# Moving the loads of pairs seven and eight behind the fourth pair's bit rows in a fused hash attention and gated MLP kernel

## The chip, the cores and the metric

The kernel runs on one core of a Trainium2 chip. The metric is the device time of one execution in microseconds, as the median of several runs. A core has a matrix engine (PE, with its weight loads shown as PEld), a vector engine (DVE), a scalar engine for activations (ACT), a general engine (POOL) and a sync engine (SP) that here issues nearly all DMA transfers. The engines run side by side, each works through its own instructions in program order, and semaphores order them against each other. The transfers themselves run on 16 DMA engines.

## The reference

There are 4 batches of 8 heads, 768 positions and 64 features. Every query and key is hashed into a bucket of six bits by the signs of six projections. A query attends only to keys in its own bucket. The result goes through a gated MLP with 512 inputs and 1536 hidden units.

```python
q_bits = (np.einsum('bhsd,dk->bhsk', q, proj) > 0).astype(np.int64)
k_bits = (np.einsum('bhsd,dk->bhsk', k, proj) > 0).astype(np.int64)
q_bucket = np.sum(q_bits * powers, axis=-1)
k_bucket = np.sum(k_bits * powers, axis=-1)
mask = q_bucket[:, :, :, None] == k_bucket[:, :, None, :]
scores = np.where(mask, scale * np.matmul(q, k.transpose(0, 1, 3, 2)), -1e9)
attn = softmax(scores)              # over the keys
attn_out = np.matmul(attn, v)
...
x = attn_out.transpose(0, 2, 1, 3).reshape(B * S, H * D)
g = x @ w_gate
gelu = 0.5 * g * (1.0 + erf(g / sqrt(2)))
ffn_out = gelu * (x @ w_val) @ w_out
out = x + sigmoid(x @ w_res) * ffn_out
```

## The kernel before, in words

**Pairs.** The 32 heads are worked on as 16 pairs, four pairs to a batch, numbered 0 to 15 in the code (so "pair seven" of the title is index 6, and "the fourth pair" is index 3). For each pair, `load` (L87) issues one transfer for the queries (side 0), one for the keys (side 1) and one for the values (side 2) from SP. Queries and keys are held in three buffers per side, so that pair 6 takes the buffer of pair 3 and pair 7 that of pair 4.

**From load to scores.** Queries and keys go two ways. On the first, `cast` (L191, POOL) makes them bf16, `transpose_dma` (L208, issued from SP) turns them so that the features lie on partitions (tile `aug`), and `move_second` (L212, POOL) copies the second head's half into the tile `second`. On the other way, `blocks` (L242, DVE) transposes the float32 data in blocks of 32 into `t32` (five buffers), and `hash_half` (L274, PE) multiplies them with the projections, in two halves of the feature dimension, into one PSUM tile. After the second half a DVE instruction (L287) turns the sums into signs. From index 4 on, two pairs are hashed together: `hash_half` of 4 covers pairs 4 and 5, that of 6 covers 6 and 7. `spread` (L293) is four DVE shuffles that bring the signs into rows, and `mask_rows` (L322) is four transfers of 10.5 KB each that lay these seven rows (the "bit rows") beside the transposed features: two into `second` and two into `aug`, in this order. The scores are then one matmul over features and bit rows together, and a bucket that differs costs so much that the exponential is nought.

**The order.** The program is written out by hand as 147 chunks ("slots"). In each, `scores` (L436) issues the score matmuls of one chunk and its exponential on ACT; then come the tasks that `at(slot, function, ...)` (L529) has put down for this slot, in the order in which they were put down; and then, by `flush`, the products with the values of the chunk two places earlier. The first pair has 12 chunks, the others have 9 each. `base(p)` is the first slot of pair p: `b1`, `b2` and `b3` in the code are the slots 12, 21 and 30, and `base(4)` is slot 39. A task's slot fixes only its place in its engine's order, and for transfers the place in SP's order; when it runs is set by semaphores.

**What follows.** Three chunks into a batch, `gate_val` (L450) does the first half of the MLP for the batch before it, in 12 steps, as one block of PE work; the second half (`project`, L475) is cut into single matmuls that fill the PE between the chunks of the next batch. The MLP weights come in by `load_w` (L175, 512 KB each, four staging buffers, issued on SP) and are cast to bf16 by `cast_w` on POOL. The first four are issued at slot b2 + 1, the next four at b3 + 1.

The tasks that the change moves are put down in the lines L636 to L674. Around them stand, in SP's order: the bit rows of pair 2, the transposes of pair 3 and the values of pair 3 (L635 to L638); the loads of pairs 6 and 7 (L639, L653); the bit rows of pair 3 (L654); the values and transposes of pair 4 (L657, L659); four weight loads (L662); the values of pair 5 (L664); the bit rows of pair 4 (L672).

Of the kernel before, what the change touches and what calls it, by code (L numbers as in the profile page):

```python
# [17 lines left out]
def kernel(  # L18
# [498 lines left out]
    def base(p):  # L517
        return order.index((p, 0))
# [10 lines left out]
    def at(slot, f, *args):  # L529
        if f in (hash_half, transpose_pe):  # L530
            uses_tp.add(slot)
        tasks[slot].append(lambda: f(*args))
        busy[slot] += cost.get(f, 0.0)
# [88 lines left out]
    b1, b2, b3 = (base(i) for i in (1, 2, 3))  # L622
# [13 lines left out]
    for side in range(2):  # L636
        at(b1 + 3, transpose_dma, (3, side))
    at(b1 + 3, load, 3, (2,))  # L638
    at(b1 + 3, load, 6, (0, 1))  # L639
    at(b1 + 2, blocks, (3, 1))  # L640
    at(b1 + 2, blocks, (4, 0))
    at(b1 + 4, blocks, (4, 1))
# [6 lines left out]
    for side in range(2):  # L649
        at(b1 + 6, move_second, (3, side))  # L650
        at(b1 + 7, cast, (5, side))
        at(b1 + 7 + side, blocks, (5, side))
    at(b1 + 7, load, 7, (0, 1))  # L653
    at(b1 + 8, mask_rows, 3)  # L654
    at(b1 + 8, values_prep, 3)

    at(b2, load, 4, (2,))  # L657
# [9 lines left out]
    for a in range(4):  # L667
        at(b2 + 6 + a // 2, spread, 4, a)

    for i, s in enumerate((b2 + 2, b2 + 7, b2 + 8, b3 + 2)):  # L670
        at(s, blocks, (6 + i // 2, i % 2))
    at(b3, mask_rows, 4)  # L672
    for dh, s in enumerate((b3 + 4, b3 + 6)):
        at(s, hash_half, 6, dh, ROW)  # L674
    for i in range(NWS):
        at(b2 + 5 + i, cast_w)
# [120 lines left out]
```

## Time and profile before

| | |
|---|---|
| median of 5 runs | 348.92 us (348.65 to 351.32) |
| time of the profiled execution | 348.92 us |
| its span, first to last instruction | 347.1 us |
| PE busy, share of the span | 335.7 us, 97% |
| ACT busy | 210.3 us, 61% |
| DVE busy | 153.2 us, 44% |
| POOL busy | 153.1 us, 44% |
| transfers issued through SP's queue | 43.56 MB, 45.3% of the 16 DMA engines |
| first scores of pairs 1, 2, 3 and 4 | about 20, 30, 40 and 50 us |

An engine that is busy in the profile is not always at its peak: the ends of the matmuls are modelled. The shares are means over stages that differ. In the first 50 us the program works on batch 0 alone and has no MLP matmuls to fill the PE with; afterwards blocks of `gate_val` (about 54 to 86 us for the first one) alternate with attention of the next batch, filled with MLP matmuls. In lines of a timeline the first number is the start in us, the second the time from the first start to the last end, and what stands in brackets is how long the engine was idle before it and what ended that. "SPq" rows are the issuing instructions on SP, not the transfers.

### The profile page before, as it was taken

To read this page: it belongs to the slowest core of one execution; us is meant where nothing else is said; L and a number is where in the kernel's file an instruction comes from. 1 tells how busy PE (TensorE), PEld (TensorE's weight loads), DVE (VectorE), ACT (ScalarE), POOL (GpSimd) and SP (SyncE) were. 2 spreads that over 40 slices of the span, in tenths; PEclk is the share of its full clock that TensorE was granted. 3 is DMA by queue.
4 is the path that set the end of the run, shared out by engine and by line. 5 is a ranking of instruction groups with operands and counts; after the bars stand their busy time and mean duration, and the time that the engine had idled before them with its cause. 6 is when DMAs were issued, how large, how long until landed. Compare 5 with 4: busy or idle time off the path is not lost.

```text
span 347.1 us, 7432 instructions
## 1 busy us (share of the span) xinstructions
PE 335.7 (97%) x2961; PEld 197.1 (57%) x3010; DVE 153.2 (44%) x280; ACT 210.3 (61%) x238; POOL 153.1 (44%) x198
## 2 busy tenths in 40 slices
PE   8999989999999999999999999999999999999995
PEld 4545656655565566566456556566556565656443
DVE  5997823334136526343444446343452025334243
ACT  5888986334898886223888788323788884332220
POOL 6898575865479496200068579300038222000000
PEclk9999999999999999999999999999999999999999
DMA  7966999896806973730014783600003321000012
GB/s 227 275 229 190 284 340 199 290 343 175 261 17 161 207 215 79 190 115 2 0 37 126 185 204 105 145 23 1 2 3 89 59 55 60 2 0 2 30 60 91
DMA packets 52718, 44.04 MB, mean 127 GB/s; under 512 B 31657, under 2 KB 44621, under 8 KB 52685
## 3 DMA queue, kind: packets, MB, share of 16 engines
q1 hardware_dynamic: 52540, 43.56, 45.3%
q8 instruction: 23, 0.38, 0.5%
q14 instruction: 11, 0.08, 0.1%
q0 software_dynamic: 64, 0.02, 0.0%
q10 hardware_dynamic: 80, 0.00, 0.0%
HBM read 29.36 MB, written 6.29 MB: 103 GB/s over the span
## 4 chain that ended last, share of the span: by engine, by line
PE 84%; ACT 4%; DVE 4%; POOL 4%; issue 2%; DMA 2%; DVEq 0%; ACTq 0%; POOLq 0%
PE sp L463 35%; PE fps L498 16%; PE sp L441 13%; PE av L412 8%; PE rps L483 5%; PE hs L282 4%; ACT e L445 4%; DMA aug<-bits 2%; PE wps L188 1%; POOL ldv L338 1%; POOL va L332 1%; DVE x_tok L389 1%; POOL o L507 1%; DVE o L504 1%; PE tp L398 1%
## 5 line engine op out<-in xcount | busy, mean ns | idle before, releaser
L445 ACT ACTIVATE e<-sp 128x1024 bf16<-128x1024 f32 (+1 forms) x147 | 143.5, 1008 | 25.5 <-PE sp L441 22.3
L469 ACT ACTIVATE gt<-sp 128x768 bf16<-128x768 f32 x48 | 38.9, 810 | 83.0 <-PE sp L463 83.0
L470 DVE SCALAR_TENSOR_TENSOR hh<-gt,sp 128x768 bf16<-128x768 bf16 x48 | 45.8, 954 | 81.4 <-PE sp L463 81.4
L498 PE MATMUL fps<-wo,hh 128*128 128x512 bf16 (+2 forms) x285 | 74.3, 369 | 1.3
L463 PE MATMUL sp<-x_sb,wg 128*128 128x256 bf16 (+1 forms) x376 | 70.3, 325 | 0.4
L463 PE MATMUL sp<-x_sb,wv 128*128 128x256 bf16 (+1 forms) x376 | 69.8, 325 | 0.6 <-DVE hh L470 0.2
L412 PEld LDWEIGHTS <-e 128*128 128x128 bf16 x1152 | 50.1, 97 | 33.2 <-issue 9.3
L441 PE MATMUL sp<-aug,aug 71*128 71x512 bf16 x192 | 54.3, 326 | 2.9 <-ACT e L445 1.7
L412 PE MATMUL av<-va,e 128*128 128x65 bf16 x1152 | 56.0, 193 | 0.6
L463 PEld LDWEIGHTS <-wv 128*128 128x128 bf16 x384 | 37.5, 98 | 25.2 <-issue 0.4
L463 PEld LDWEIGHTS <-wg 128*128 128x128 bf16 x384 | 37.2, 98 | 24.4
L441 PE MATMUL sp<-second,second 128*128 128x256 bf16 (+1 forms) x174 | 47.4, 320 | 0.2
L507 POOL TENSOR_TENSOR o<-o,x_tok 128x512 f32<-128x512 f32 x18 | 20.8, 1155 | 56.2 <-DVE o L504 49.3
L498 PEld LDWEIGHTS <-hh 128*128 128x128 bf16 x300 | 28.6, 97 | 27.0
L504 DVE SCALAR_TENSOR_TENSOR o<-th,fps 128x512 f32<-128x512 f32 (+2 forms) x25 | 16.5, 662 | 52.9 <-PE fps L498 34.7
L389 POOL TENSOR_TENSOR x_tok<-total,rec 128x768 bf16<-128x768 f32 x9 | 13.2, 1472 | 45.0 <-DVE rec L388 45.0
L214 POOL COPY second<-aug 64x768 bf16<-64x768 bf16 x29 | 23.6, 825 | 19.5 <-DMA aug<-nat 17.8
L245 DVE STREAM_TRANSPOSE t<-ld 128x768 f32<-128x768 f32 (+1 forms) x34 | 29.5, 904 | 3.7 <-DMA ld<-in_q_dram 2.2
L486 ACT ACTIVATE th<-rps 128x512 f32<-128x512 f32 x24 | 14.3, 596 | 18.7 <-PE rps L483 14.3
L483 PE MATMUL rps<-wr,x_sb 128*128 128x512 bf16 x96 | 24.6, 379 | 0.0
L441 PEld LDWEIGHTS <-second 128*128 128x128 bf16 x192 | 18.6, 98 | 5.3 <-issue 2.3
L441 PEld LDWEIGHTS <-aug 71*128 71x128 bf16 x192 | 16.2, 97 | 6.6 <-issue 1.8
(71 smaller groups left out, 233.8 us busy)
## 6 DMA issues: line engine op xcount, KB each, us to landing
ldv<-in_v_dram SPq DMA_DIRECT2D x16, 384.0 KB
out_dram<-o SPq DMA_DIRECT2D x23, 256.0 KB
ld<-in_q_dram SPq DMA_DIRECT2D x15, 384.0 KB
ld<-in_k_dram SPq DMA_DIRECT2D x15, 384.0 KB
ws<-in_moe_w_gate_dram SPq DMA_DIRECT2D x6, 512.0 KB
ws<-in_moe_w_val_dram SPq DMA_DIRECT2D x6, 512.0 KB
ws<-in_moe_w_out_dram SPq DMA_DIRECT2D x6, 512.0 KB
ws<-in_moe_w_res_dram SPq DMA_DIRECT2D x2, 512.0 KB
```

What stands on the lines that cost most here:

```text
L214: eng.tensor_copy(second[x[0] % NM][x[1]][D:P], aug[x][D:P])
L245: nc.vector.transpose(t32[x][:, c0:c1].rearrange("p c h n -> p (c h n)"), raw[x][:, c0:c1].rearrange("p c d -> p (c d)"))
L412: nc.tensor.matmul(o[:, qt0 + i, :], e[:, off + i * P:off + (i + 1) * P], va[:, hi, jt, 0:D + 1], start=(hi not in begun), stop=(jt == T - ...
L441: nc.tensor.matmul(sp[:, off:off + nq * P], ks[0:n, jt, :], qs[0:n, qt0:qt0 + nq, :], start=True, stop=True)
L445: nc.scalar.activation(e[:, 0:n], sp[:, 0:n], AF.Exp, scale=float(ALPHA))
L463: nc.tensor.matmul(sp[:, c0:c1], w[:, kk, bass.ts(m, P)], xs[:, kk, c0:c1], start=(kk == 0), stop=(kk == KM - 1))
L469: nc.scalar.activation(gt, sp[:, 0:S], AF.Gelu)
L470: nc.vector.scalar_tensor_tensor(hh[:, m, :], gt, 0.5, ps[1][:, 0:S], op0=ALU.mult, op1=ALU.mult)
L483: nc.tensor.matmul(rps, x_sb[b][:, kk, t, :], wr[:, kk, :], start=(kk == 0), stop=(kk == KM - 1))
L498: nc.tensor.matmul(fps, hh[:, m, bass.ts(t, P)], wo[:, m, cs], start=(m == 0), stop=(m == KF - 1))
L504: nc.vector.scalar_tensor_tensor(o[:, cs], th[:, cs], 1.0, fps, op0=ALU.add, op1=ALU.mult)
L507: last.tensor_add(o3, o3, x_tok[b][:, k0:k1, t, :])
```

## The change

Three things are put in other places; no instruction is added or taken away. (1) The loads of queries and keys of pair 6 (they stood at slot b1 + 3) and of pair 7 (at b1 + 7) are both put at b1 + 8, and the bit rows of pair 3 move from b1 + 8 to b1 + 7, so that on SP they are issued ahead of these four loads. (2) The four `blocks` of pairs 6 and 7 move from the slots b2 + 2, b2 + 7, b2 + 8 and b3 + 2 to b2 + 6, b2 + 8, b3 + 2 and b3 + 3. (3) The two hash halves of pairs 6 and 7 move from b3 + 4 and b3 + 6 to b3 + 5 and b3 + 7.

```diff
@@ -636,7 +636,6 @@
     for side in range(2):
         at(b1 + 3, transpose_dma, (3, side))
     at(b1 + 3, load, 3, (2,))
-    at(b1 + 3, load, 6, (0, 1))
     at(b1 + 2, blocks, (3, 1))
     at(b1 + 2, blocks, (4, 0))
     at(b1 + 4, blocks, (4, 1))
@@ -650,8 +649,9 @@
         at(b1 + 6, move_second, (3, side))
         at(b1 + 7, cast, (5, side))
         at(b1 + 7 + side, blocks, (5, side))
-    at(b1 + 7, load, 7, (0, 1))
-    at(b1 + 8, mask_rows, 3)
+    at(b1 + 7, mask_rows, 3)
+    for i in (6, 7):
+        at(b1 + 8, load, i, (0, 1))
     at(b1 + 8, values_prep, 3)
 
     at(b2, load, 4, (2,))
@@ -667,10 +667,10 @@
     for a in range(4):
         at(b2 + 6 + a // 2, spread, 4, a)
 
-    for i, s in enumerate((b2 + 2, b2 + 7, b2 + 8, b3 + 2)):
+    for i, s in enumerate((b2 + 6, b2 + 8, b3 + 2, b3 + 3)):
         at(s, blocks, (6 + i // 2, i % 2))
     at(b3, mask_rows, 4)
-    for dh, s in enumerate((b3 + 4, b3 + 6)):
+    for dh, s in enumerate((b3 + 5, b3 + 7)):
         at(s, hash_half, 6, dh, ROW)
     for i in range(NWS):
         at(b2 + 5 + i, cast_w)
```

## The prediction, before the change was run

> **What bounds the kernel now.** I read the page first, then the chain of waits, then the queue and engine timelines around 20 to 60 us, where every edit lies. The profiled execution took 348.92 us, the same as the median of the five runs shown; 347.1 us of it is the span. The sum below is made against 348.92.
>
> The page, with its 40 slices of 8.68 us:
>
> ```profile
> span 347.1 us, 7432 instructions
> ...
> DMA  7966999896806973730014783600003321000012
> ```
>
> The DMA engines are 90% busy in the slices from 34.7 to 60.7 us and little used after 60. PE has only 6.8 us of gaps in the whole span (gaps between its rows added up), so from the first MLP stage (about 54 us) on it is full: a stall of PE before that is not won back later, it moves the end one to one. The question is therefore what decides when batch 0 is over. The chain of waits between 9 and 60 us (start, us, what):
>
> ```profile
> 40.53 0.59 PE sp L441 x2
> 41.13 0.26 PE av L412 x8
> 41.39 0.84 POOL second L214
> ...
> 44.64 5.34 DMA aug<-bits
> 49.98 0.05 issue
> 50.03 0.62 PE sp L441 x2
> ```
>
> Until 40 us the chain runs through the exponentials on ACT. Then it leaves the engines: the fifth pair (index 4) cannot begin its scores before its bit rows have landed, and this small transfer, issued at 44.64, lands at 49.98. The engines around it:
>
> ```profile
> 50.03 0.39 PE L441 MATMUL sp<-aug,aug 71*128 71x512 bf16 x1 [0.73 <-DMA aug<-bits]
> ```
> ```profile
> 50.73 2.86 ACT L445 ACTIVATE e<-sp 128x1024 bf16<-128x1024 f32 x3 [0.56 <-PE sp L441]
> ```
> ```profile
> 40.62 1.59 POOL L214 COPY second<-aug 64x768 bf16<-64x768 bf16 x2 [3.82 <-DMA aug<-nat]
> ```
>
> PE stands 0.73 us, ACT 0.56 us. So at this one place the DMA queue is already the bound, by 0.56 us. Why does a 10.5 KB transfer take 5.34 us? By SP's timeline four weight loads of 512 KB (issued 39.32 to 41.4) and a value load lie ahead of it, and these lie behind the two transposes, and these behind the loads that the change moves:
>
> ```profile
> 29.82 0.59 SPq L95 DMA_DIRECT2D ldv<-in_v_dram  x1
> 30.46 0.46 SPq L95 DMA_DIRECT2D ld<-in_q_dram  x1
> 31.02 0.41 SPq L95 DMA_DIRECT2D ld<-in_k_dram  x1
> 31.54 0.40 SPq L95 DMA_DIRECT2D ld<-in_q_dram  x1
> 32.04 0.41 SPq L95 DMA_DIRECT2D ld<-in_k_dram  x1
> 32.54 1.51 SPq L329 DMA_DIRECT2D second<-bits  x2
> 34.16 1.48 SPq L329 DMA_DIRECT2D aug<-bits  x2
> 35.69 0.44 SPq L95 DMA_DIRECT2D ldv<-in_v_dram  x1
> 36.69 2.58 SPq L209 DMA_TRANSPOSE aug<-nat  x2
> ```
>
> The stretches (last columns: DMA share, GB/s) show that from 32 us on the engines never run dry:
>
> ```profile
> 31.00:32.00 1.00, 0.87 (x13) 0.60 (x11) 1.00 (x2) 1.00 (x2) 0.64 (x1) 1.00 0.74 152
> 32.00:33.00 1.00, 1.00 (x10) 0.29 (x8) 0.97 (x3) 1.00 (x2) 0.91 (x2) 1.00 1.09 394
> 33.00:34.00 1.00, 1.00 (x9) 0.29 (x8) 0.70 (x1) 0.36 (x1) 1.00 (x3) 1.00 1.00 369
> ```
>
> The trace's semaphore increments tell when each transfer landed (median of its engines): value load 33.0, loads of pair 6 at 34.0 and 35.0, of pair 7 at 36.3 and 37.4, pair 3's bit rows by 38.3, value load of pair 4 39.56, transposes 40.4 and 41.2, weights 43.0 to 47.1, value load 48.2, bit rows of pair 4 49.0 (their last engine 49.98). It is one line of work from 32 to 50.
>
> **The change, part by part.**
>
> Loads behind the bit rows of pair 3. SP issues the same four loads and four bit-row transfers, in the other order; SP's own time is unchanged. The bit rows need the last of four shuffles, which ends at 30.85 (DVE, 30.50 + 0.35), and the copies of the second head, which end at 30.95 and 32.18 (POOL); the second kind gates only the two aug transfers. Four took 32.54 to 35.64, 3.10 us, so now 30.95 to 34.05. The first load is issued at 34.1 instead of 30.46, the value load at 36.1 and the transposes at 36.6, as before. But the DMA engines have nothing large between 33.3 and the first bytes of that load. The nearest row is the value load issued at 18.21 on an empty queue: it landed at 21.3, 3.07 later. So pair 6's first load lands at 37.2; the next loads follow at 1.02 each (22.32, 23.34, 24.36, 25.36 in the same burst): 38.2, 39.2, 40.2, the value load of pair 4 at 41.25 instead of 39.56. **Late by 1.7 us**; at the 1.12 us that the four loads took here (34.04 to 37.40) by 2.0. Part may come back: between the transposes (41.2) and the first weight load (43.0) lie 1.9 us where the later weight loads are 1.34 apart, so 0.4 to 0.5 us are dry there now, and with a queue that is behind they would be filled. That gives 1.3 at least, 2.0 at most; I take **1.6 us**, near the middle, as nothing speaks for either end.
>
> What is late next: the transposes land at 42.1 instead of 40.4, POOL's copies (40.62) follow, behind them on POOL pair 4's values (42.28 to 45.25) and the weight casts, each 1.6 later. First use of these values is after the scores of pair 4, which are late too. The second group of weights is cast by 57.4; its first use is the fifth of twelve MLP steps, about 53.8 + 4 x 2.6 = 64.2: 7 us of cover. Without it 1.6 us would be paid again. Bit rows of pair 4 land at about 51.6, and PE starts that pair at 51.65 instead of 50.03.
>
> Bit rows of pair 3 1.6 us earlier: worth nothing. They landed by 38.4, and pair 3 starts at 40.53 in a row of nine exponentials without a pause (36.62 to 45.07).
>
> Blocks later. Four DVE transposes of 0.92, same number. One wait goes:
>
> ```profile
> 35.60 0.98 DVE L245 STREAM_TRANSPOSE t<-ld 128x768 f32<-128x768 f32 x1 [1.90 <-DMA ld<-in_q_dram]
> ```
>
> Behind it stood the sign step of pairs 4 and 5 (36.50), whose matmuls had ended at 35.72, so up to 0.8 us is gained there; now a block stands between two pairs of shuffles, 0.92 lost. The shuffles still end near 39.6, and SP reaches pair 4's bit rows at 42.21. I take 0; the cover is 2.6 us, and without it -0.8 to +0.9.
>
> Hash halves one chunk later: eight matmuls each, 0.78. The first half now falls into the chunk that also holds six PE transposes (0.5). ACT stands 0.49 and 0.54 us at 45.55 and 48.13 after the halves now. This could save both or double both: -1.0 to +1.0, all before the bit rows land, with the last exponential of pair 3 ending at 50.17 against bit rows at 51.6. I take 0, covered by 1.4. The hash itself is used by shuffles a whole pair later.
>
> Sum: 348.92 + 1.6 = **350.5 us**, PE's gap at that pair 0.73 + 1.6 = 2.3 us.
>
> The granted clock is 1.00 in every one of these stretches, beside a gap of 0.73 us. The Trainium skill's TensorE page (TensorE: Matmul & The Clock Gate, section Why this matters for your kernels) warns against PE gaps over about 3 us, after which the clock is halved. The gap worked out here stays under that, so by the rule the sum is the same; only the deep case below would cross it, and by the rule another 1.7 us (an estimate: half of a 3.4 us window) would come on top there. No gap here is that long, so the trace can't confirm it.
>
> **Rivals.**
>
> 1. *The delay is taken up.* All of the dry time before the weights is refilled (the 1.3 above), and the one DMA engine that makes the bit rows land 1.0 us after the other six (49.98 against 49.05) falls elsewhere: 1.3 - 1.0 = +0.3: 349.2. For it: such late engines come and go (loads at 34.04 had one engine at 35.58). Against: the weight stream is full, and nothing says where the late one falls.
>
> 2. *Deeper.* A late engine adds to the hole. After an instruction fetch of 16 KB that took 1.04 us on one engine, that engine's share of the next five loads was 1.0 to 1.5 late. If the bit rows sit on one that is late by this more than now, 1.6 + 1.0 to 1.5 = 2.6 to 3.1: **351.8 us**. It decides if the last of the bit rows lands after 52.5.
>
> 3. *Faster.* The load's delay is hidden and the shorter waits on DVE and ACT count: bit rows land before 50.0, ACT goes straight on at 50.17, saving its 0.56, and the two pauses of 0.49 and 0.54 go with the moved hash: 348.92 - 1.6 = 347.3 at best, 348.4 with the first alone. It decides only if the queue is not behind at all at 41 us, and the landings above say that it is.
>
> That the order on SP doesn't change is excluded: one queue, in program order.
>
> **How the numbers follow.** Forecast 0.52, its own range 349.9 to 351.2; taken up 0.17; deeper 0.23; faster 0.08. What a measurement of this kernel can tell is about 0.5%, 1.74 us: 347.2 and 350.66. Slower than that: four tenths of the forecast's case and the deep one, 0.22 + 0.23 = 0.45. Faster: half of the last, 0.05 with rounding. The rest, 0.50, is the same. Range 348.9 to 351.9: it leaves out the faster case and the upper half of the deep one.
>
> **What would show it.** Right: on SP the four bit-row transfers start near 31 and the first of the four loads near 34; DMA share well under 0.5 from 34 to 36; POOL's copies of pair 4 near 42.3; PE's wait for aug<-bits at pair 4 near 2.3 us at 51.6; the gate and value matmuls start 1.6 later and everything behind them by the same. Wrong in size: a wait of another length there. Wrong in kind: no wait for bit rows at pair 4, or a difference that arises after 60 us; also DVE waiting for a load again, which would make the hash late.

## The result, and the profile after

The changed kernel is slower: a median of 352.59 us over 23 runs, against 348.82 us over 44 runs of the kernel before. The ratio of the two kernels on record is 1.0081, with a 95% interval of 1.0061 to 1.0102, that is 2.8 us (2.1 to 3.6). The medians lie further apart, 3.8 us: the changed kernel's executions took longer where their granted clock was lower (348.6 to 349.9 us at 0.998 or more, 352.7 and more at 0.990), and the two slowest, 355.21 and 355.73 us, are not in the ratio. Its profiled execution took 351.38 us with a span of 349.6.

First the head of the page of the changed kernel and the rows of its 40 slices (8.74 us each) for the granted clock and the DMA engines:

```profile
span 349.6 us, 7430 instructions
...
PEclk9999998999999999999999999999999999999999
DMA  7965999798724972850003793510002311000012
```

The fourth DMA slice (26 to 35 us) has 5 where the kernel before had 6, and the seventh slice of the clock, 52 to 61 us, shows 8 instead of 9. The kernel before shows 9 in every slice of the clock. Next the chain of waits between 30 and 60 us (start, us, what):

```profile
35.20 8.39 DMA aug<-nat
...
43.74 0.61 POOL second L214
...
44.51 0.84 POOL second L214
...
47.68 4.00 DMA aug<-bits
...
51.73 0.93 PE sp L441 x2
```

In the kernel before the chain ran through ACT until 40 us. Now it leaves ACT at 35.2 and goes through the transposes of pair 4, the copies, and the bit rows of pair 4. The engines at the same place, PE first, then ACT, then POOL:

```profile
51.73 0.50 PE L441 MATMUL sp<-aug,aug 71*128 71x512 bf16 x1 [3.67 <-DMA aug<-bits]
```
```profile
52.76 1.02 ACT L445 ACTIVATE e<-sp 128x1024 bf16<-128x1024 f32 x1 [3.82 <-PE sp L441]
```
```profile
43.74 1.59 POOL L214 COPY second<-aug 64x768 bf16<-64x768 bf16 x2 [8.01 <-DMA aug<-nat]
```

PE's wait for the bit rows of pair 4 has grown from 0.73 to 3.67 us, and POOL's for the transposes from 3.82 to 8.01. SP's queue shows the new order:

```profile
29.45 1.49 SPq L329 DMA_DIRECT2D second<-bits  x2
31.05 1.50 SPq L329 DMA_DIRECT2D aug<-bits  x2
32.60 0.44 SPq L95 DMA_DIRECT2D ld<-in_q_dram  x1
33.10 0.45 SPq L95 DMA_DIRECT2D ld<-in_k_dram  x1
33.59 0.47 SPq L95 DMA_DIRECT2D ld<-in_q_dram  x1
34.11 0.47 SPq L95 DMA_DIRECT2D ld<-in_k_dram  x1
34.62 0.47 SPq L95 DMA_DIRECT2D ldv<-in_v_dram  x1
35.20 6.22 SPq L209 DMA_TRANSPOSE aug<-nat  x2
```

And the stretches of 1 us (last three columns: granted clock, DMA share, GB/s):

```profile
32.00:33.00 1.00, 1.00 (x21) 0.73 (x20) 0.00 (x0) 0.76 (x2) 1.00 (x3) 1.00 0.04 11
33.00:34.00 1.00, 1.00 (x12) 0.16 (x8) 0.00 (x0) 0.80 (x2) 0.91 (x2) 1.00 0.38 58
...
37.00:38.00 1.00, 1.00 (x16) 0.79 (x13) 1.00 (x4) 1.00 (x3) 0.00 (x0) 1.00 0.86 192
38.00:39.00 1.00, 0.91 (x13) 0.50 (x10) 1.00 (x5) 1.00 (x3) 0.00 (x0) 1.00 0.79 221
...
41.00:42.00 1.00, 0.94 (x18) 0.63 (x18) 1.00 (x3) 1.00 (x2) 0.00 (x0) 1.00 0.58 39
42.00:43.00 1.00, 0.92 (x13) 0.65 (x12) 0.91 (x2) 1.00 (x2) 0.00 (x0) 1.00 0.53 112
...
52.00:53.00 1.00, 1.00 (x12) 0.70 (x11) 0.00 (x0) 0.24 (x1) 0.30 (x1) 0.50 1.07 414
```

There are two holes in the DMA stream where the kernel before had one line of work: the expected one at 32 to 34 us, where the loads have not been issued yet, and a second at 41 to 43; at 37 to 39 the stream is slower too. The half clock begins as PE's gap ends and lasts from 51.9 to 55.3.

**Where the time went.** The two profiles start differently (pair 1's first exponential is at 20.71 before and at 19.76 after, which no part of the change touches), so I count from that exponential. The first Gelu comes 35.43 us after it before and 39.01 us after it now: +3.58. From the first Gelu to the end it is 291.00 and 290.83 us. Thus 3.58 - 0.95 - 0.17 = 2.46 us, which is the difference of the spans, and all of the loss lies ahead of the first Gelu.

### The profile page after: what moved, and what is told of

It reads as the page before. It is cut to its first block, busy times and chain, and to the rows that moved or that the text cites. A ratio compares the mean times of both kernels' runs of the same rounds, so it can differ in the third digit from the quotient of the medians.

```text
span 349.6 us, 7430 instructions
## 1 busy us (share of the span) xinstructions
PE 334.8 (96%) x2961; PEld 197.2 (56%) x3010; DVE 153.3 (44%) x280; ACT 210.1 (60%) x238; POOL 153.0 (44%) x198
## 4 chain that ended last, share of the span: by engine, by line
PE 81%; DMA 5%; POOL 4%; ACT 3%; DVE 3%; issue 2%; SPq 0%; POOLq 0%; DVEq 0%; ACTq 0%
PE sp L463 35%; PE fps L498 15%; PE sp L441 13%; PE av L412 8%; PE rps L483 5%; PE hs L282 4%; ACT e L445 3%; DMA aug<-nat 2%; DMA aug<-bits 1%; DMA ld<-in_q_dram 1%; POOL ldv L338 1%; POOL va L332 1%; DVE x_tok L389 1%; POOL o L507 1%; POOL second L214 1%
## 5 line engine op out<-in xcount | busy, mean ns | idle before, releaser
L445 ACT ACTIVATE e<-sp 128x1024 bf16<-128x1024 f32 (+1 forms) x147 | 143.3, 1008 | 29.3 <-PE sp L441 24.7
L412 PEld LDWEIGHTS <-e 128*128 128x128 bf16 x1152 | 50.8, 98 | 33.3 <-issue 9.4
L463 PEld LDWEIGHTS <-wv 128*128 128x128 bf16 x384 | 37.6, 98 | 25.2 <-issue 0.3
```

Source lines behind the costliest of these rows:

```text
L412: nc.tensor.matmul(o[:, qt0 + i, :], e[:, off + i * P:off + (i + 1) * P], va[:, hi, jt, 0:D + 1], start=(hi not in begun), stop=(jt == T - ...
L445: nc.scalar.activation(e[:, 0:n], sp[:, 0:n], AF.Exp, scale=float(ALPHA))
L463: nc.tensor.matmul(sp[:, c0:c1], w[:, kk, bass.ts(m, P)], xs[:, kk, c0:c1], start=(kk == 0), stop=(kk == KM - 1))
```

## The experiments

HOLE is the theory that the late loads leave the DMA engines empty, so that the transposes and bit rows of pair 4 come late and PE's clock drops after the wait. TASKS is the rival that the moved blocks and hash halves do it. "Gelu" is the time in us from pair 1's first exponential to the first Gelu in the profile, "gap" the longest idle time of PE, in us, between 30 and 55 us of the profile and what ended it.

| run | ratio to before, 95% | Gelu | gap |
|---|---|---|---|
| before | 1 | 35.43 | 0.73, bit rows of pair 4 |
| changed | 1.0081 (1.0061 to 1.0102) | 39.01 | 3.67, bit rows of pair 4 |
| e1 loads only | 1.0074 (1.0046 to 1.0102) | 39.06 | 2.08, division of pair 2 |
| e2 blocks and hash only | 0.9991 (0.9965 to 1.0017) | 35.30 | 0.90, exponential on ACT (bit rows of pair 4 landed just then, too) |
| e3 only pair 7's loads late | 0.9990 (0.9965 to 1.0015) | 35.21 | 0.81, bit rows of pair 4 |
| e4 filler | 1.0064 (1.0040 to 1.0089) | 37.71 | 0.47, exponential on ACT |
| e5 changed, bits first | 0.9997 (0.9974 to 1.0020) | 35.09 | 0.32 |
| e6 changed, transposes first | 1.0076 (1.0041 to 1.0110) | 37.71 | 1.57, division of pair 2 |
| e7 before, bits first | 0.9993 (0.9968 to 1.0017) | 35.18 | 0.89, bit rows of pair 3 |
| e8 changed, both first | 1.0021 (0.9997 to 1.0045) | 37.53 | 1.52, division of pair 2 |
| e9 e8 with later blocks | 0.9952 (0.9928 to 0.9976) | 34.37 | 0.32 |
| e10 e6 with later blocks | 1.0068 (1.0036 to 1.0100) | 38.54 | 2.95, bit rows of pair 4 |
| e11 e7 with the change's blocks | 0.9984 (0.9961 to 1.0007) | 35.38 | 0.85, bit rows of pair 3 |
| e12 changed, bits from POOL | 1.0084 (1.0056 to 1.0113) | 40.45 | 3.65, bit rows of pair 3 |

### e1 and e2: the change in its two halves

e1 is the changed kernel with

```diff
-    for i, s in enumerate((b2 + 6, b2 + 8, b3 + 2, b3 + 3)):
+    for i, s in enumerate((b2 + 2, b2 + 7, b2 + 8, b3 + 2)):
...
-    for dh, s in enumerate((b3 + 5, b3 + 7)):
+    for dh, s in enumerate((b3 + 4, b3 + 6)):
```

and e2 is the kernel before with this edit turned round.

> Only the loads are moved behind the bit rows of pair 3; blocks and hash halves stand where they stood before. Theory HOLE (the DMA engines run empty ahead of the late loads, so the transposes, weight loads and bit rows of pair 4 land late, and PE then stands so long that its clock falls): as slow as the whole change, +2.8 to +3.8 us on the kernel before, with a wait of PE for aug<-bits at pair 4 of 3 to 4 us. Rival TASKS (the later blocks and hash halves push the chunks of pair 3 back): at most +0.5 us. One thing could add to it: the block of pair 6 again waits on DVE for its load, about 4 us, with pair 4's sign step behind it; the bit rows of pair 4 are issued later than that, so HOLE expects no cost from it.

> Only the blocks and the hash halves of pairs 6 and 7 are moved; the loads stay in front. HOLE: the same time as before within 0.5 us, PE's wait at pair 4 again 0.5 to 1.0 us. TASKS: slower by 2 us or more.

The loads alone lose as much as the whole change, the blocks and hash halves alone lose nothing that can be told: TASKS falls. But in e1 the loss sits in another place than HOLE said. DVE waits for pair 6's load, and behind it stands the division of pair 2, which frees the accumulator that pair 3's products need. DVE's rows of e1, then PE's:

```profile
36.05 0.98 DVE L245 STREAM_TRANSPOSE t<-ld 128x768 f32<-128x768 f32 x1 [4.07 <-DMA ld<-in_q_dram]
...
42.41 0.96 DVE L389 TENSOR_TENSOR x_tok<-av,rec 128x768 bf16<-128x768 f32 x1
```
```profile
43.51 1.04 PE L412 MATMUL av<-va,e 128*128 128x65 bf16 x16 [2.08 <-DVE x_tok L389]
```

This gap of 2.08 us costs more than itself, for the clock is at 0.50 from 42.4 to 49.3 us. The bit rows of pair 4 landed at 52.31 in e1 and PE came to them at 52.5, so there was no wait left. One lateness on two paths: with the blocks in their old place the late load holds PE by way of DVE, with the blocks later it holds it by way of the bit rows. The two do not add up, for the second hides behind the first.

### e3: half of the loads

The changed kernel with the loads of pair 6 in front again:

```diff
     at(b1 + 3, load, 3, (2,))
+    at(b1 + 3, load, 6, (0, 1))
...
-    for i in (6, 7):
-        at(b1 + 8, load, i, (0, 1))
+    at(b1 + 8, load, 7, (0, 1))
```

> The whole change, but the loads of pair 6 go back in front of pair 3's bit rows (slot b1 + 3); only those of pair 7 stay behind them. HOLE: the loads of pair 6 keep the DMA engines busy until about 35, those of pair 7 are issued at 34.6 and would land at 37.7 on an empty queue against 36.3 before, so the hole is 1.0 to 1.5 us instead of 2 to 3.4: +0.2 to +1.5 us on the kernel before, PE's wait at pair 4 between 0.7 and 2.2 us, clock whole. If the order against the bit rows as such counted, and not the empty stretch, it would be half of the change's loss or more: +1.4 us up.

The loss is gone, not halved. The transposes of pair 4 still landed 1.1 us later than before (20.84 against 19.73 us after the first exponential), but the bit rows 0.2 us earlier. The first 1.1 us of lateness are taken up on the way (dry time ahead of the weights, one late DMA engine), as the prediction's first rival had it; only what is over that arrives.

### e4: the clock

```diff
+        if (p, c) == (HP, 0):
+            warm_up(14, 4)
         new = scores(p, c)
```

> The whole change, with 14 matmuls of 512 columns on constants (3.0 us at full clock, results not used) put in front of the first scores of pair 4, where PE stands for 3.67 us. If the halved clock after that gap costs what the rows of the changed kernel say (52 to 56 us at 0.50, first Gelu 7.0 us after the pair's first score against 6.1 before), this is 0.9 us faster than the changed kernel, its granted clock is 1.00 throughout, and the wait for aug<-bits shrinks by the 3 us while the pair starts at the same time. If the clock costs nothing (ACT being the bound there), it is the same as the changed kernel within 0.3 us.

PE's rows of e4 show the filler, and the wait behind it:

```profile
47.93 3.19 PE L188 MATMUL wps<-eps_sb 128*128 128x512 bf16 x14
51.40 0.39 PE L441 MATMUL sp<-aug,aug 71*128 71x512 bf16 x1 [0.28 <-DMA aug<-bits]
```

The clock is 1.00 throughout. From PE's first score of pair 4 to the first Gelu it is 6.11 us, as in the kernel before, against 7.04 in the changed one: the half clock costs **0.93 us** there, in this pair of profiles. The rest of the 1.3 us that e4's Gelu is earlier is a bit row that landed earlier in this execution. The medians (351.15 against 352.59) point the same way; the intervals of the two ratios overlap.

### e5 and e7: the bit rows of pair 4 ahead of 1.4 MB

In the changed kernel (e5) and in the one before (e7):

```diff
-    for i in range(NWS):
+    for i in range(2):
         at(b2 + 1, load_w)
...
-    at(b2 + 6, load, 5, (2,))
...
     at(b3, mask_rows, 4)
+    for i in range(2):
+        at(b3, load_w)
+    at(b3, load, 5, (2,))
...
-        at(b2 + 5 + i, cast_w)
-        at(b3 + 1, load_w)
+        at((b2 + 5, b2 + 6, b3 + 2, b3 + 3)[i], cast_w)
+        at(b3 + 1 + i // 2 * 3, load_w)
```

> The whole change, and the bit rows of pair 4 are issued ahead of two of the four weight loads (the value side's) and of the values of pair 5, so that 1.4 MB less lies in front of them; these loads and their casts come behind, and the second group's value side behind pair 5's transposes. Theory HOLE says that the loads of pairs 6 and 7 cost only by way of these bit rows: they land about 3.3 us earlier (48.4 against 51.7 in the changed kernel's profile), PE's wait at pair 4 falls from 3.7 to under 0.6 us, the clock stays whole, and the time is 3.5 to 4.2 us below the changed kernel, -0.5 to +0.3 us on the kernel before. If the late loads cost by another way too (pair 6's data, POOL, the weights), 1 us or more of the loss stays.

> The kernel before, with the same reordering of pair 4's bit rows ahead of two weight loads and pair 5's values. If the bit rows hold PE in the kernel before as well (0.73 us, ACT 0.56), they now land near 46, the wait is gone and the time is 0.3 to 0.8 us lower; if the later weight loads come too late for the first gate matmuls, it is higher by what PE waits there, up to 2 us.

e5 is HOLE's plainest test: the loads are as late as in the change, and the loss is gone. In the changed kernel, with its blocks later, they cost by way of pair 4's bit rows; beside e7, which has the same edit with the loads early (0.9997 and 0.9993), a cost by another way can't be told. The profile alone is less clear, for behind the first Gelu it is 0.7 us longer than before (291.69 against 291.00), and no run here tells why. ACT's rows of e5 go through pair 4's start (49.36, four exponentials in a row) after 0.65 us of idle time where the changed kernel has 3.82:

```profile
46.77 1.94 ACT L445 ACTIVATE e<-sp 128x1024 bf16<-128x1024 f32 x2 [0.67 <-PE sp L441]
49.36 3.97 ACT L445 ACTIVATE e<-sp 128x1024 bf16<-128x1024 f32 x4 [0.65 <-PE sp L441]
```

e7 took the wait at pair 4 away too, but the gain can't be told from nothing. In its profile PE waits one pair earlier, for the bit rows of pair 3, which lie behind the early loads:

```profile
39.06 0.38 PE L441 MATMUL sp<-aug,aug 71*128 71x512 bf16 x1 [0.89 <-DMA aug<-bits]
```

So the old order can have a cost of its own. In the profile shown of before it was not there.

### e6, e8, e9 and e10: the transposes of pair 4 ahead of the late loads

e6 is the changed kernel with

```diff
+    for side in range(2):
+        at(b1 + 8, transpose_dma, (4, side))
     for i in (6, 7):
         at(b1 + 8, load, i, (0, 1))
...
-        at(b2, transpose_dma, (4, side))
```

and e8 is e6 with the edit of e5.

> The whole change, with the two transposes of pair 4 issued ahead of the four late loads, into the empty stretch, and not behind them. The bytes ahead of pair 4's bit rows are the same. HOLE with the transposes as a barrier (they begin only when the last engine has done what lies before them, 1.5 us of nearly empty engines in the changed kernel): transposes land near 36 instead of 44, no engine waits for a late one, bit rows near 49.6 instead of 51.7, PE's wait 1.5 us instead of 3.7, clock whole: 2.5 to 3.2 us below the changed kernel, +0.2 to +1.0 on the kernel before. If the barrier costs nothing and only the bytes and the hole count: the hole is filled by the transposes anyhow, but loads start 2.6 us later still; bit rows as in the changed kernel, time within 0.7 us of it.

> The whole change with both: pair 4's transposes ahead of the late loads and its bit rows ahead of two weight loads and pair 5's values. HOLE: no wait for bit rows at pair 4, so the same as the kernel before with the bit rows first, -0.8 to 0 us on the kernel before, whatever the loads of pairs 6 and 7 do. If their lateness matters elsewhere, it is the same as the other one of the changed kernel with the bit rows first.

The transposes landed at 37.6 in e6 and the bit rows of pair 4 at 51.48, when PE came to them; there is no wait for them in either. The times missed what I expected, for the reason that e1 had shown: the loads are issued 2.7 us later still, the block of pair 6 waits for its load on DVE even in its later place, and the division of pair 2 behind it is late. PE and the stretches of e6:

```profile
43.84 0.99 PE L412 MATMUL av<-va,e 128*128 128x65 bf16 x16 [1.57 <-DVE x_tok L389]
```
```profile
42.00:43.00 1.00, 0.28 (x2) 0.00 (x0) 0.97 (x3) 1.00 (x2) 0.00 (x0) 1.00 1.02 360
43.00:44.00 1.00, 0.16 (x5) 0.19 (x6) 1.00 (x2) 0.46 (x1) 0.00 (x0) 0.96 1.01 352
44.00:45.00 1.00, 1.00 (x17) 0.78 (x15) 1.00 (x2) 0.00 (x0) 0.00 (x0) 0.50 1.06 383
```

A gap of 1.57 us is followed by half a clock. e9 (from e8) and e10 (from e6) put the blocks behind that division:

```diff
-    for i, s in enumerate((b2 + 6, b2 + 8, b3 + 2, b3 + 3)):
+    for i, s in enumerate((b3 + 2, b3 + 3, b3 + 4, b3 + 5)):
...
-    for dh, s in enumerate((b3 + 5, b3 + 7)):
+    for dh, s in enumerate((b3 + 7, b3 + 8)):
```

> The changed kernel with pair 4's transposes ahead of the late loads, its bit rows ahead of two weight loads and pair 5's values, and in addition the four blocks of pairs 6 and 7 at b3 + 2 to b3 + 5 and their hash halves at b3 + 7 and b3 + 8, behind the division of pair 2 on DVE. The version without the last step had a PE gap of 1.52 us at 41.9 (the products of pair 3 with the values wait for pair 2's division, which stands on DVE behind a block that waits for its load) and a halved clock after it. Expected: that gap and the half clock are gone, no wait for bit rows, first Gelu 35.0 to 35.3 us after the first exponential of pair 1 (35.4 in the kernel before), -0.5 to +0.2 us on the kernel before. If the DVE order was not the cause, the gap stays near 1.5 and the time near +0.7.

> The changed kernel with pair 4's transposes ahead of the late loads and the same later blocks and hash halves; its bit rows stay behind all four weight loads. HOLE with the transposes as a barrier: the bit rows land 30.9 us after the first exponential of pair 1, as in the version with the earlier blocks, against 31.9 in the changed kernel, though the loads are issued 2.7 us later; PE waits 2 to 2.7 us for them, the clock is halved afterwards, first Gelu 37.5 to 38.1 us after that exponential against 39.0: 0.7 to 1.5 us below the changed kernel. If only bytes and hole counted, the bit rows would land 2.7 us later than in the changed kernel and it would be slower than that by 2 us or more.

e9 has neither wait and beats both kernels: 347.13 us median, ratio 0.9952 (0.9928 to 0.9976), 1.7 us below the kernel before, more than expected. ACT's row runs from pair 2 through most of pair 3:

```profile
35.57 11.23 ACT L445 ACTIVATE e<-sp 128x1024 bf16<-128x1024 f32 x12 [0.25 <-PE sp L441]
```

e10 came in between: bit rows 31.3 us after the first exponential (30.9 expected, 31.9 in the changed kernel), though its loads were issued 2.7 us later than the changed kernel's; first Gelu at 38.54, later than expected. Its time can't be told from the changed kernel's. The 2.7 us that bytes and hole alone were expected to add are too many, for the transposes no longer lie between the loads and the bit rows, which spares 1.5 us there (they landed from 42.78 to 44.25 in the changed kernel). But that still makes 1.2 us later, and the bit rows came 0.6 earlier. So what the changed kernel loses at 41 to 43 us belongs to the transposes' place behind the loads.

### e11 and e12: two misses

e11 is e7 with the later blocks and hash halves of the change. e12 is the changed kernel with

```diff
-    at(b1 + 7, mask_rows, 3)
+    at(b1 + 7, mask_rows, 3, (nc.gpsimd, nc.gpsimd))
```

> The kernel before with its loads in front, the bit rows of pair 4 ahead of two weight loads and pair 5's values, and the later blocks and hash halves of the change. Each alone gave nothing that could be told (the first kept a DVE wait for pair 6's load with a PE gap of 0.89). Together: no gap over 0.4 us between 30 and 52, first Gelu 34.4 to 34.8 us after the first exponential of pair 1 against 35.4, -0.6 to -1.0 us on the kernel before.

> The whole change, but the four bit-row transfers of pair 3 are issued from POOL's queue instead of SP's. SP then goes from pair 3's values straight to the four loads, 3.1 us earlier, in the same program order. HOLE: no empty stretch of the DMA engines, so the time of the kernel before within 0.5 us and PE's wait at pair 4 under 1.5 us with a whole clock; POOL's four issues (about 0.6 each) delay pair 3's values and nothing else. If the loads' place against the bit rows in DMA order were the cause, the loss of 2.8 us stays.

In e11 the DVE wait is gone, but PE's gap of 0.85 us stayed: I had put e7's gap down to DVE, and it was the bit rows of pair 3. In e12 the hole did go, loads landing at 33.5 to 37.4 and pair 4's bit rows 29.3 us after the first exponential, just as before the change. The time stayed, as the loss moved to pair 3. POOL issues its bit rows only at 33.46, behind two casts and behind the loads, and PE waits for them:

```profile
42.42 0.39 PE L441 MATMUL sp<-aug,aug 71*128 71x512 bf16 x1 [3.65 <-DMA aug<-bits]
```

So in e12 small transfers lost their place behind large ones at pair 3; the changed kernel lets that happen at pair 4.

## Why the prediction was right in kind and short in size

The prediction put the one place right (the bit rows of pair 4), the path to it (hole, transposes, copies, bit rows) and the sign, and its range of 348.9 to 351.9 holds the 351.6 us that the ratio makes of 348.82, though neither the changed kernel's median (352.59) nor the upper end of the interval (352.4). Its likeliest case, 350.5 and within what can be told from no change, was too small: +1.6 forecast, +2.8 measured (2.1 to 3.6), +3.58 in the profile counted from pair 1's first exponential. Step by step, as lateness against the kernel before counted from that exponential (landings by the semaphore increments, the median of the 16 engines; bit rows by their last):

| step | predicted | measured |
|---|---|---|
| first load of pair 6 landed | +3.2 | +2.6 |
| value load of pair 4 landed | +1.7 (to 2.0) | +4.2 |
| first weight load landed | +1.3 to 2.0 | +3.6 |
| last bit row of pair 4 landed | +1.6 | +2.7 |
| PE starts pair 4 | +1.6 | +2.7 |
| first Gelu | +1.6 | +3.6 |

**The hole** was sized nearly right. It is 32 to 34 us in the stretches, and the first late load landed 3.05 us after its issue (3.07 was taken). That it was 0.6 us less late than forecast comes from the bit rows of pair 3, which SP issued 0.55 us earlier, counted from the first exponential, than the prediction had them.

**The step that failed is the chain from there to pair 4's value load.** The prediction let the loads follow each other at 1.02 us each. From the first landing at 35.66 that gives 39.74 for the value load; it landed at 42.78, 3.0 us later. Of these, 1.0 came up at the keys of pair 7, which landed at 39.72 instead of 38.72: at 37 to 39 us the engines moved only 192 and 221 GB/s, and single packets of 1.5 KB took up to 2.07 us. The other 2.0 came up at the value load itself. Pair 7's queries had landed by 38.3 on fourteen of the 16 engines, on one at 39.07 and on the last at 40.75, the last share of the keys came at 41.80, and then the value load landed on all 16 engines at once, at 42.73 to 42.83. Meanwhile the transposes that stand behind could not go on: packets of theirs that started at 40.3 to 41.3 took 1.3 to 2.4 us each and all ended at 42.62 to 42.66, and the engines moved 39 GB/s at 41 to 42. The prediction's second rival had named a late engine, but as something that hits the bit rows at the end; by these traces it acts earlier, at the transposes. The late engine was no accident of one execution: e1 has it (the same load, last engine at 41.26, others by 38 to 39), e4 too (40.45), and in the kernel before the last engine of the same four loads was 1.2 to 1.6 us late (the second rival has 1.0 to 1.5). Why an engine is late, and why by more behind the hole, is open; no run here tells.

**Taken back**: 0.6 us ahead of the weights (4.2 to 3.6), close to the 0.4 to 0.5 that the prediction had counted, and 0.9 more because the engine that delayed the bit rows by 1.0 us before did not do so now. The prediction had this second part only in its first rival; it hides part of what the value load cost, and that the range held is in this part luck.

**The clock** was counted at nothing, at a gap of 2.3 us. The gap was 3.67, and e4 shows the half clock to cost 0.93 us. Together with the 2.65 us by which PE starts pair 4 later these are the 3.58 of the profile. The Trainium skill's TensorE page (TensorE: Matmul & The Clock Gate, section Why this matters for your kernels) warns of gaps over about 3 us. The runs here disagree with that bound: with gaps of 1.52 (e8), 1.57 (e6) and 2.08 us (e1) the clock fell to 0.50 as well. So the gap of 2.3 that was forecast need not have been safe either.

**Blocks and hash halves at nothing**: right (e2). The cover that was named, SP's late arrival at pair 4's bit rows, was not what mattered. What the move changes is seen in e1: without it DVE waits for the late load with pair 2's division behind it. In time it bought nothing (1.0081 against 1.0074 in e1), for the bit rows of pair 4 were as late. The prediction looked only at the sign step behind that wait.

**Bit rows of pair 3 earlier at nothing**: right for the profile shown, but in e7 and e11, which have the loads in their old place, these bit rows held PE for 0.85 to 0.89 us. A gain of that kind is possible, and it would be far smaller than what the late loads cost.

**A line read wrongly**: the prediction calls the DMA engines little used after 60 us. The row that it shows has 8, 9, 6 and 8 for the slices from 60.7 to 95.5 us. Nothing in its sum rests on this.

## What to carry to other kernels

A transfer that nobody waits for still holds a place in the queue. Before it is moved, follow what is issued behind it down to the first small transfer that an engine does wait for, and put that one ahead of the bulk rather than pushing the bulk back: this alone took the loss away in e5, and with the transposes ahead and the blocks behind it made e9 faster than the kernel before. Where two paths are late by the same cause, undoing one shows nothing, for the other takes over (e1, e8 against e9). And a stall on PE should be priced with the clock that follows it.

## What the runs showed of the hardware that was not expected

- DMA transposes seem to act as a barrier over the 16 engines (read from the traces; the order was tried in e10, the barrier not by itself). In the changed kernel the stream sank to 39 GB/s while one engine still carried out loads issued ahead of them, the waiting packets of the transpose all ended within 0.04 us, and the issue of the second transpose on SP took 4.6 us instead of 1.2. In the kernel before it is there in small: such packets started at 38.66 to 38.97 us and ended at 39.46 to 39.50, just before the value load ahead of them landed. In e6, e8, e9 and e10, with the transposes ahead of the loads, none of their packets took over 0.5 us.
- PE's clock fell to half with gaps of 1.52, 1.57, 2.08, 2.95, 3.65 and 3.67 us, for 3.4 us each time and for 6.8 in e1 and e12, and not with gaps of 0.73 to 0.90. The moment does not follow the gap: in e1 and e8 it fell about 1 us into the gap, in e10 only 1.7 us after PE had begun again. In all six runs it fell a whole number of times 3.41 us after it had first risen to 1.00 (14 times in the changed kernel, at 4.09 and 51.88 us; 11 times in e1, at 4.88 and 42.43). So where a gap lies against this beat seems to count beside its length; no run here moves a gap to try it.
